# Fixed rows for the tokens routed last, and plain stores of the last output block

## The chip, the core and the metric

The kernel runs on one core of a Trainium2 chip. The core has five engines with an instruction queue each, and each queue runs strictly in order: TensorE (PE, matrix products), VectorE (DVE), ScalarE (ACT), GpSimd (POOL) and SyncE (SP, which here issues transfers). Engines wait for one another, and for transfers, by semaphores. The metric is the device time of one execution in microseconds (us); lower is better.

## The reference, cut to what matters

Attention over 4 sequences of 576 tokens, then a feed-forward in which each token goes to one of 8 experts, then a dense feed-forward with a squared relu. The 2304 output rows stand in the order of the tokens.

```python
x = attention(q, k, v, bias)                  # 2304 tokens x 512
expert_idx = np.argmax(logits, axis=1)        # one of 8 experts a token
for e in range(E):
    mask = expert_idx == e
    h = np.maximum(x[mask] @ w1[e], 0.0)
    out[mask] = gate_w[mask, None] * (h @ w2[e])
h = out @ w_in                                # 512 -> 2048
r = np.maximum(h, 0.0)
return (r * r) @ w_out                        # 2048 -> 512, 2304 rows
```

## The kernel before

**Stages.** Attention goes over 18 tiles of 128 tokens (`TILES`; the two last in the list are the tiles of chunk 3 of sequences 2 and 3). When a batch of tiles is done, `route` ranks its tokens within their experts and POOL scatters the token numbers into a list by expert, `id_d`. `base` holds the running count of tokens for each expert. `slots` cuts the list into slots of 128 tokens of one expert: 7 early slots (`NEARLY`) from the first 14 tiles, and then slots 7 to 21 (the compiled most is 30; what lies above 22 stands in a branch that these inputs don't take).

**The loop over slots** (`run_slots`, some 11 us a slot). For each slot POOL gathers the token numbers (`gather_id`, into `ti`), later the rows of x (`gather_x`, into `xg`), and splits x in two halves of 16 bits (`x_split`). PE transposes (`x_T`), multiplies with the expert's first matrix (`ff1`, two halves), and with the second (`ff2`). After each half of `ff1`, ACT and DVE make `h2` (DVE's line is L1226), and where the next slot has another expert they split new weights (`split_w1`). Between these stand the pieces of `convert`, which turns the dense weights into 16-bit pairs on ACT, DVE and POOL. The order on each engine is the order in which the code is written. In step `t` the code emits `gather_id(t + 6)`, `gather_x(t + 4)`, `ff1(t + 1)`, `x_T(t + 2)`, `x_split(t + 3)` and `ff2(t)`, in that order.

**Where a slot's results go.** `ff2_out` appends two numbers to each result row, a factor and the token's place in the output, and `y_out` stores the rows to `y_d`: early slots by SP in a plain transfer, later ones by POOL in an indirect transfer to the rows `yidx`, which closes the gaps that half-filled slots leave. So which token stands in which row of `y_d` depends on the data, and each row carries its place in the output with it.

**The dense feed-forward** goes over 9 blocks of 256 rows of `y_d`. `y_load` fetches them, `y_rows` takes out the factor (`meta`) and the place (`orow`), `g_unit` makes the hidden layer, and `ff2_of` the output in seven products of 24 matmuls into the PSUM tiles a, b, c, d. From these ACT and DVE (`comb`, L1465) put together two output tiles `o[0]` and `o[1]` of 128 rows x 512. `put` has POOL store each in an indirect transfer to the rows `orow` of the result (L1469):

```python
w = POOL.indirect_dma_start(out=out, out_offset=bass.IndirectOffsetOnAxis(ap=orow[:, t:t + 1], axis=0),
                            in_=o[i], in_offset=None, bounds_check=NT - 1, oob_is_err=False).ins
```

**The end of the program** (all under L1585): every engine runs a DRAIN and signals; SP first waits for the semaphore of every transfer; POOL collects the signals, clears the semaphores, and releases all.

Of the kernel before, what the change touches and what calls it, by code (L numbers as in the profile page):

```python
# [7 lines left out]
F32 = mybir.dt.float32  # L8
F16 = mybir.dt.float16
U32 = mybir.dt.uint32  # L10
I32 = mybir.dt.int32
AF = mybir.ActivationFunctionType
ALU = mybir.AluOpType
# [3 lines left out]

B, H, S, D = 4, 8, 576, 64
HID = 32
STEP, LIM = 1.95, 2.7  # L20
NT, DM = B * S, H * D
E, F1 = 8, 1024
F2 = 2048
P = 128
NP = H // 2
TILES = [(c, b) for c in (0, 1, 4, 2, 3) for b in ((0, 2) if c == 4 else range(B))]
NTILE = len(TILES)
NSLOT = NT // P + E - 1
NEARLY, TEARLY, NMOST = 7, 14, 22
XW, XX = DM + 2, DM + 3  # L30
# [53 lines left out]
def body(ctx: ExitStack, tc: tile.TileContext, q, k, v, wsm, emb, tau, mw1, mw2, win, wout, cst_d, lsk_d, ids_d, out):  # L84
    nc = tc.nc
    win, wout = win.bitcast(U32), wout.bitcast(U32)
    PE, ACT, DVE, POOL, SP = nc.tensor, nc.scalar, nc.vector, nc.gpsimd, nc.sync

    dram = ctx.enter_context(tc.tile_pool(name="dram", bufs=1, space=DRAM))
    cp = ctx.enter_context(tc.tile_pool(name="cp", bufs=1))  # L90
# [6 lines left out]
    x_d = dram.tile([NT + P, XX], F32, name="x_d")  # L97
# [11 lines left out]
    orow = cp.tile([P, NTILE], U32, name="orow")  # L109
    base = cp.tile([P, E], F32, name="base")  # L110
# [2 lines left out]
    w2s_c = cp.tile([P, 1], F32, name="w2s_c")  # L113
    basep = cp.tile([P, E], F32, name="basep")
    taken = cp.tile([P, E], F32, name="taken")
    xidx = cp.tile([P, NSLOT], U32, name="xidx")
    yidx = cp.tile([P, NSLOT], U32, name="yidx")
    tok = cp.tile([P, NTILE], U32, name="tok")
# [8 lines left out]
    def attention(actx, bctx, cctx, smp, mid, early, G):  # L127
        ap = lambda n, bufs, **kw: actx.enter_context(tc.tile_pool(name=n, bufs=bufs, side="right", **kw))
# [33 lines left out]
        def start(g, tag="B"):  # L162
            active.append([g, E_, tag])
# [460 lines left out]
        def route(bat):  # L624
            R = rbat.pop(bat)
            n = len(R["x"])
# [12 lines left out]
            ti = T("ti")  # L639
# [4 lines left out]
            z = T("z", E)  # L644
# [34 lines left out]
            if bat == (2, 0):  # L679
                DVE.tensor_copy(basep, base)  # L680
                start(early(), "A")
            ACT.activation(z, z, AF.Exp)
            yield E_
            DVE.tensor_tensor(out=rr, in0=rr, in1=oh, op=ALU.mult)
# [12 lines left out]
            for i, ti_ in enumerate(R["x"]):  # L697
                if i and (i == 2 or not soon):
                    yield E_

                put = POOL.indirect_dma_start(out=id_d, out_offset=bass.IndirectOffsetOnAxis(ap=ri[:, i:i + 1], axis=0),
                                              in_=tok[:, ti_:ti_ + 1], in_offset=None, bounds_check=E * NT * IW - 1,
                                              oob_is_err=False).ins
# [92 lines left out]
        for n in range(8, GR):  # L796
            c, i = divmod(n, 8)
# [61 lines left out]
    def slots(pool, fin):  # L859
        t0, n = (NEARLY, NSLOT - NEARLY) if fin else (0, NEARLY)  # L860
        tl = lambda shape, nm: pool.tile([P] + shape, F32, name="sl_" + nm)
        tn = lambda shape, nm: pool.tile([P, NSLOT - NEARLY] + shape, F32, name="sl_" + nm)[:, :n]
        ev8 = cst[:, C_E2304:C_E2304 + E]
# [3 lines left out]
        pcol = cst[:, C_P:C_P + 1]  # L867
        bc = lambda a: a.unsqueeze(1).to_broadcast([P, n, E])

        def below(x, nm):  # L870
            t2 = tl([E, E], "t2")
            DVE.tensor_tensor(out=t2, in0=x.unsqueeze(1).to_broadcast([P, E, E]), in1=tri8, op=ALU.mult)
            r = tl([E], nm)
            DVE.tensor_reduce(out=r, in_=t2, axis=AX.X, op=ALU.add)
            return r

        rem = tl([E], "rem")
# [23 lines left out]
        a = max(t0, 1)  # L901
# [31 lines left out]
            return  # L933

        DVE.tensor_scalar(live_i, cin[:, E - 1:E], float(NEARLY), None, op0=ALU.add)
        D = below(rem, "D")
        c128 = tl([E], "c128")
        DVE.tensor_scalar(c128, cex, float(P), None, op0=ALU.mult)
# [5 lines left out]
        DVE.tensor_scalar(tp, tt[:, :, 0], float(P), pcol, op0=ALU.mult, op1=ALU.add)  # L944
        DVE.tensor_tensor(out=R, in0=R, in1=tp, op=ALU.is_gt)
        DVE.scalar_tensor_tensor(out=Y, in0=tt[:, :, 0], scalar=float(P), in1=Y, op0=ALU.mult, op1=ALU.add)
        DVE.scalar_tensor_tensor(out=Y, in0=Y, scalar=float(NEARLY * P - NT), in1=R, op0=ALU.add, op1=ALU.mult)
        DVE.tensor_scalar(Y, Y, float(NT), pcol, op0=ALU.add, op1=ALU.add)
        DVE.tensor_copy(yidx[:, t0:t0 + n], Y)

    with tc.manual_schedule():
# [32 lines left out]
        def gather_x(t):  # L984
            a = G["xg"].tile([P, XX], F32, name="xg")
            n = TEARLY * P if t < NEARLY else NT + P
            POOL.indirect_dma_start(out=a, out_offset=None, in_=x_d[0:n, :],
                                    in_offset=bass.IndirectOffsetOnAxis(ap=ids.pop(t)[:, 0:1], axis=0),
                                    bounds_check=n - 1, oob_is_err=False)
            xg[t] = a  # L990

        def slot(t):
            ev[t] = SP.value_load(es_i[0:1, t:t + 1], min_val=0, max_val=E - 1)
# [53 lines left out]
        def early():  # L1047
            while "one" not in G:
                yield E_
            loaded = False  # L1050

            def first_loads():
                load_slot(0)

            for i, _ in enumerate(slots(G["one"], False)):
                if i > 3 and not loaded and "xs" in G:
                    first_loads()
                    loaded = True
                if i % 2:
                    yield E_  # L1060
            while "ids" not in G:
                yield E_
            gather_id(0)
            gather_id(1)
            while "xs" not in G:
                yield E_
            if not loaded:
                first_loads()
            yield E_
            gather_id(2)  # L1070
            gather_id(3)
            while "x" not in G:
                yield E_
            yield E_
            gather_x(0)
            gather_x(1)
            yield E_
            gather_x(2)
            gather_id(4)
            gather_id(5)  # L1080
            yield E_
            for kc in range(4):
                yield E_
                split_part(0, kc // 2, kc % 2)
                if kc < 3:
                    x_split(kc)
            while G["hs"] < HSW:
                yield E_
            for kc in range(4):
                load_w2(0, kc, True)  # L1090
            yield E_
            load_slot(1)
            turn(1, NMOST)
            yield E_
            load_slot(2)
# [162 lines left out]

        def y_rows(i, yr):
            DVE.tensor_copy(meta[:, i, :], yr[:, DM:XW])  # L1260
            DVE.tensor_copy(orow[:, i:i + 1], yr[:, DM + 1:XW])


        conv = pieces([convert(i, wrp) for i in range(NCONV)])
# [118 lines left out]
        with ExitStack() as fctx:  # L1383
# [64 lines left out]
            def ff2_of(j):  # L1448
                gt = gts.pop(j)
                m = [meta[:, 2 * j + i, 0:1] for i in range(2)]  # L1450
                bank = [pf2.tile([P, 512], F32, name=f"pf2_{x}")[:, :256] for x in "abcd"]
                pa, pb, pc, pd = bank
                o = [op_.tile([P, DM], F32, name=f"o{i}") for i in range(2)]
                u = lambda nm: up.tile([P, 256], F32, name=nm)

                def prod(ps, s, w, first, end):
                    i = 0
                    for c in range(8):
                        for a, b in ((0, 0), (0, 1), (1, 0)):
                            PE.matmul(ps, lhsT=gt[:, a, s, c, :], rhs=woh[:, c, b, w, :],  # L1460
                                      start=(i == 0 and first), stop=(i == 23 and end), skip_group_check=True)
                            i += 1

                def comb(dst, ps, i, x):
                    DVE.scalar_tensor_tensor(out=dst, in0=ps, scalar=m[i], in1=x, op0=ALU.mult, op1=ALU.add)  # L1465

                def put(i):
                    t = 2 * j + i
                    w = POOL.indirect_dma_start(out=out, out_offset=bass.IndirectOffsetOnAxis(ap=orow[:, t:t + 1], axis=0),  # L1469
                                                in_=o[i], in_offset=None, bounds_check=NT - 1, oob_is_err=False).ins  # L1470
                    for other in outs:
                        tc.declare_no_dep(w, other, reason="disjoint rows")
                    outs.append(w)

                prod(pa, 0, 0, True, False)
                s = [u(f"s{i}") for i in range(2)]
                for i in range(2):
                    ACT.activation(s[i], pa, AF.Copy, scale=m[i])
                yield
                prod(pb, 4, 4, True, True)  # L1480
                u2 = [u(f"u{i}") for i in range(2)]
                for i in range(2):
                    comb(u2[i], pb, i, s[i])
                yield
                prod(pc, 3, 3, True, False)
                u4 = u("u4")
                comb(u4, pc, 0, u2[0])
                yield
                prod(pd, 5, 5, True, False)
                comb(o[0][:, 256:], pd, 0, u4)  # L1490
                yield
                prod(pa, 2, 2, False, True)
                ACT.activation(o[1][:, :256], pa, AF.Copy, scale=m[1])  # L1493
                yield
                prod(pc, 6, 1, False, True)
                comb(o[1][:, 256:], pc, 1, u2[1])
                put(1)
                yield
                prod(pd, 1, 6, False, True)
                comb(o[0][:, :256], pd, 0, u2[0])  # L1500
                put(0)
                yield

            for g in range(8):
# [85 lines left out]
```

## Time and profile before

| | us |
|---|---|
| median of 3 runs (1011.03 to 1012.91) | 1011.57 |
| the profiled execution | 1017.84 |
| its span, first to last instruction | 1016.0 |
| PE, DVE, ACT, POOL busy in the span | 947.2, 662.3, 540.9, 497.0 |

The page gives busy times by engine, a chain of work that ended last, and groups of instructions; the trace behind it can be asked for a stretch, a line or an engine. DRAIN and semaphore instructions belong to an engine's sequencer (POOLq, SPq) and are not counted as busy, so a wait at the very end is not in the busy times. Instructions are named by line of the kernel before; a "releaser" is what ended an engine's idle time.

### The profile page before, as it was taken

The page shows a single profiled execution, that of the slowest core. Times are in us where ns is not written, and L with a number is a line of the kernel's source. Part 1 is how long each engine was busy: PE and PEld are TensorE (multiplying, and loading weights), DVE is VectorE, ACT ScalarE, POOL GpSimd, SP SyncE. Part 2 cuts the span into 40 slices and gives each one's busy share as a digit, 9 for nine tenths or more (in the row PEclk, how much of TensorE's full clock was granted, in tenths as well). Part 3 has the DMA queues.
Part 4 walks back from the last instruction along what each step waited for, and adds up shares of the span by engine and source line. Part 5 has one row for each costly group of instructions (what it writes and reads, how often), then busy time and mean ns, then how long its engine had stood idle before and what let it go on. Part 6 is the DMA issues. An engine that isn't in the chain of part 4 may idle for free. (4 is left out here: it accounts for less than half of the span.)

```text
span 1016.0 us, 24944 instructions
## 1 busy us (share of the span) xinstructions
PE 947.2 (93%) x9725; PEld 749.5 (74%) x9725; DVE 662.3 (65%) x1229; ACT 540.9 (53%) x1000; POOL 497.0 (49%) x415
## 2 busy tenths in 40 slices
PE   8687999999899879999989999999999999999995
PEld 4456776677577658777657667688888888888884
DVE  6665999988988664677866867245445455545441
ACT  6666777777777574455756665255323333333330
POOL 1213536437433352456637787266454554645541
PEclk9798999999999999999999999999999999999998
DMA  9988985998779343698898574362111111111001
GB/s 299 329 242 265 327 276 174 303 267 265 242 228 326 137 125 108 229 336 300 336 410 318 196 271 170 143 275 50 25 53 43 32 52 43 32 53 22 22 1 42
DMA packets 78844, 187.18 MB, mean 184 GB/s; under 512 B 26648, under 2 KB 26776, under 8 KB 76128
## 3 DMA queue, kind: packets, MB, share of 16 engines
q1 hardware_dynamic: 72656, 169.98, 50.1%
q0 software_dynamic: 6064, 15.54, 4.6%
q8 instruction: 78, 1.28, 0.6%
q14 instruction: 46, 0.38, 0.1%
HBM read 171.65 MB, written 51.73 MB: 220 GB/s over the span
## 5 line engine op out<-in xcount | busy, mean ns | idle before, releaser
L1438 POOL TENSOR_TENSOR gf<-gf 128x256 f32<-128x256 f32 x144 | 165.9, 1171 | 146.5 <-DVE gf L1435 124.5
L1422 PE MATMUL pf<-big,wih 128*128 128x256 f16 x1728 | 196.0, 273 | 1.7 <-PEq L1376 1.7
L1422 PEld LDWEIGHTS <-wih 128*128 128x128 f16 x1728 | 169.0, 98 | 21.6 <-issue 2.1
L1460 PEld LDWEIGHTS <-g 128*128 128x128 f16 x1512 | 147.4, 98 | 18.7 <-issue 1.0
L1428 ACT ACTIVATE gf<-pf 128x512 f32<-128x512 f32 x72 | 42.5, 597 | 193.5 <-PE pf L1422 135.7
L1220 PE MATMUL ph<-x,w1b 128*128 128x128 f16 x2112 | 125.6, 219 | 4.6 <-ACT x L1204 2.4
L1220 PEld LDWEIGHTS <-w1b 128*128 128x128 f16 x2112 | 120.6, 98 | 9.5 <-issue 4.4
L471 POOL TENSOR_TENSOR wh<-wr,w2s_c 128x1024 f16<-128x1024 f32 x32 | 61.4, 1918 | 132.4 <-DMA wr<-in_mw_dram 83.1
L1235 PE MATMUL py<-vt,h 128*128 128x512 f16 x528 | 119.0, 382 | 6.1 <-DMA vt<-wsc 6.1
L1446 DVE TENSOR_TENSOR g<-gf,g 128x1792 f16<-128x1792 f32 x36 | 85.5, 2375 | 50.2 <-ACT g L1445 50.2
L522 ACT ACTIVATE pr<-ssb,mn 128x576 f32<-128x576 f32 x144 | 111.8, 777 | 11.9 <-DVE mn L509 11.7
L509 DVE CUSTOM_DVE_ANT_0 ssb<-ps_s,bias 128x576 f32<-128x576 f32 x144 | 107.5, 749 | 4.6 <-DMA bias<-bias_d 2.5
L498 PE MATMUL ps_s<-kst,qd 128*128 128x288 f16 (+1 forms) x640 | 96.4, 291 | 14.0 <-DVE mn L509 9.5
L1435 DVE TENSOR_TENSOR gf<-gf 128x1024 f32<-128x1024 f32 x28 | 34.3, 1225 | 113.6 <-ACT gf L1428 113.6
L1235 PEld LDWEIGHTS <-h 128*128 128x128 f16 x528 | 51.1, 98 | 65.0 <-issue 8.6
L531 PE MATMUL ps_t<-cst,pr 128*128 128x128 f32 x576 | 92.7, 284 | 1.3 <-DVE pt L209 0.6
L556 PE MATMUL pv<-pt,vt 128*64 128x128 f32 (+1 forms) x1280 | 85.1, 276 | 8.0 <-DMA vt<-in_v_dram 5.7
L556 PEld LDWEIGHTS pv<-pt,vt 128*64 128x64 f32 x1280 | 67.6, 141 | 24.4 <-issue 18.2
L531 PEld LDWEIGHTS ps_t<-cst,pr 128*128 128x128 f32 x576 | 65.3, 145 | 24.8 <-issue 19.7
L498 PEld LDWEIGHTS <-qd 128*128 128x128 f16 (+1 forms) x640 | 56.4, 101 | 29.1 <-issue 18.5
L207 ACT COPY pt<-ps_t 128x512 f32<-128x512 f32 x99 | 57.1, 577 | 14.9 <-PE ps_t L531 11.0
L1445 ACT CAST g<-gf 128x1792 f16<-128x1792 f32 x36 | 60.3, 1676 | 4.3 <-POOL gf L1438 4.3
(194 smaller groups left out, 1547.8 us busy)
## 6 DMA issues: line engine op xcount, KB each, us to landing
vt<-wsc SPq DMA_DIRECT2D x88, 512.0 KB
wr<-in_mw_dram SPq DMA_DIRECT2D x76, 512.0 KB
kst<-in_mw_dram SPq DMA_DIRECT2D x44, 512.0 KB
wsc<-wh SPq DMA_DIRECT2D x32, 512.0 KB
bias<-bias_d SPq DMA_DIRECT2D x16, 576.0 KB
bias_d<-rt SPq DMA_DIRECT2D x28, 295.5 KB
qd<-qh SPq DMA_DIRECT2D x64, 128.0 KB
wr<-in_win_dram SPq DMA_DIRECT2D x8, 1024.0 KB
```

The source lines that it names most:

```text
L471: POOL.tensor_tensor(out=wh[:, 0], in0=wr, in1=w2s_c.to_broadcast([P, 1024]), op=ALU.mult)
L498: PE.matmul(s[r, hf, :288], lhsT=qd[:, h2, i, pr, r], rhs=kst[x - x % 2][:, pr, h2, x % 2, js], start=(i == 0), stop=(i == 1))
L509: DVE.tensor_tensor_reduce(out=ss.rearrange("p (a j) -> p a j", a=2), in0=s[:, :, :288], in1=btile[bkey[u]][:, h2].rearrange("p (a j) -> p ...
L522: ACT.activation(pr_sb[k_ // 2][:, h2], ssb.pop(k_), AF.Exp, bias=mns.pop(k_), scale=-1.0, accum_out=sums[c, b][:, h:h + 1])
L531: PE.transpose(pt_ps[k_][:, jc * P:(jc + 1) * P], src[:, j0:j0 + P], eye)
L556: PE.matmul(pv[o, cs], lhsT=vb[:, 2 * jc + h2, d] if jc < 4 else vb[o, 8, d], rhs=a[h2][:, jc, cs] if jc < 4 else e[o, cs], start=(jc == 0 ...
L1220: PE.matmul(p_[:, f4, :], lhsT=w[:, a, kc, f * P:(f + 1) * P], rhs=x2[:, b, kc, :], start=(i == 0), stop=(i == 11))
L1235: PE.matmul(p_, lhsT=h2[:, a, fc, :], rhs=wb2[fc // 2][:, b, fc % 2, :], start=(i == 0), stop=(i == 23))
L1422: PE.matmul(p_[:, h], lhsT=wih[:, a, kc, f * P:(f + 1) * P], rhs=y2[:, b, kc, :], start=(i == 0), stop=(i == 11))
L1438: POOL.tensor_tensor(out=g[:, d], in0=g[:, x], in1=g[:, y], op=op)
L1446: DVE.tensor_tensor(out=gt[:, 1, :, c:c + 2, :], in0=g[:, 1:8], in1=gt[:, 0, :, c:c + 2, :], op=ALU.subtract)
L1460: PE.matmul(ps, lhsT=gt[:, a, s, c, :], rhs=woh[:, c, b, w, :], start=(i == 0 and first), stop=(i == 23 and end), skip_group_check=True)
```

## The change

The 256 tokens of the two tiles routed last (`ZROW` is 2048, the row where they begin) keep fixed rows: token number `ti` goes to row `ti` of `y_d`. All other tokens close their gaps among themselves, for which `slots` counts them with `basez`, the counts before the last batch, in place of `base`. The number of the row is mended slot by slot: two DVE instructions behind each `gather_x` of slots 7 and on take `max(yidx, ti if ti >= ZROW else 0)`. Since the last block's rows are then known when the program is built, `put` stores that block's two tiles with SP in four plain transfers of 128 rows x 256, each as soon as its half is ready; the other eight blocks are scattered by POOL as before.

```diff
+            if bat == (3, 0):
+                DVE.tensor_copy(basez, base)
...
         DVE.tensor_scalar(live_i, cin[:, E - 1:E], float(NEARLY), None, op0=ALU.add)
+        DVE.scalar_tensor_tensor(out=rem, in0=taken, scalar=-float(P), in1=basez, op0=ALU.mult, op1=ALU.add)
+        DVE.tensor_tensor(out=rem, in0=rem, in1=ev8, op=ALU.subtract)
...
-        DVE.scalar_tensor_tensor(out=Y, in0=Y, scalar=float(NEARLY * P - NT), in1=R, op0=ALU.add, op1=ALU.mult)
-        DVE.tensor_scalar(Y, Y, float(NT), pcol, op0=ALU.add, op1=ALU.add)
+        DVE.tensor_scalar(Y, Y, float(NEARLY * P), pcol, op0=ALU.add, op1=ALU.add)
+        DVE.tensor_tensor(out=Y, in0=Y, in1=R, op=ALU.mult)
...
             xg[t] = a
+            if t >= NEARLY:
+                z, y = zid[:, t:t + 1], yidx[:, t:t + 1]
+                DVE.scalar_tensor_tensor(out=z, in0=ti, scalar=float(ZROW), in1=ti, op0=ALU.is_ge, op1=ALU.mult)
+                DVE.tensor_tensor(out=y, in0=y, in1=z, op=ALU.max)
...
-            DVE.tensor_copy(orow[:, i:i + 1], yr[:, DM + 1:XW])
+            if i * P < ZROW:
+                DVE.tensor_copy(orow[:, i:i + 1], yr[:, DM + 1:XW])
...
-                def put(i):
+                def put(i, ns=None):
                     t = 2 * j + i
+                    if t * P >= ZROW:
+                        ch, b = TILES[t]
+                        r0 = b * S + ch * P
+                        for n in (0, 1) if ns is None else (ns,):
+                            w = SP.dma_start(out=out[r0:r0 + P, 256 * n:256 * n + 256], in_=o[i][:, 256 * n:256 * n + 256]).ins
+                            for other in outs:
+                                tc.declare_no_dep(w, other, reason="disjoint rows")
+                        return
+                    if ns == 1:
+                        return
...
                 comb(o[0][:, 256:], pd, 0, u4)
+                put(0, 1)
...
                 comb(o[0][:, :256], pd, 0, u2[0])
-                put(0)
+                put(0, 0)
```

Three places show what moved. In the rows below, the line is that of the kernel it is taken from; in brackets stand the semaphores waited for, DMASW for a transfer that POOL issued, DMAHW for one that SP issued, the rest for an engine.

The end of POOL's queue before, behind its last arithmetic (`gf`, L1438): four scatters of 128 output rows, of block 7 and of block 8, then the common end.

```order
L1438 TENSOR_TENSOR gf<-gf 128x256
L1438 TENSOR_TENSOR gf<-gf 128x256 [waits Pool_49]
L1469 DMA out_dram<-o_14870,orow 2304x512 [waits DMASW4_49,DVE_49,Activation_49]
L1469 DMA out_dram<-o_14869,orow 2304x512 [waits DMASW5_49,DVE_49]
L1469 DMA out_dram<-o_15219,orow 2304x512 [waits DMASW6_49,DVE_49,Activation_49]
L1469 DMA out_dram<-o_15218,orow 2304x512 [waits DMASW7_49,DVE_49]
L1585 UNCONDITIONAL_BRANCH
L1585 ISA [waits barrier_Pool_Activation_PE_DVE_SP_gather]
```

The same place now:

```order
L1450 TENSOR_TENSOR gf<-gf 128x256
L1450 TENSOR_TENSOR gf<-gf 128x256 [waits Pool_49]
L1491 DMA out_dram<-o_14909,orow 2304x512 [waits DMASW4_49,DVE_49,Activation_49]
L1491 DMA out_dram<-o_14908,orow 2304x512 [waits DMASW5_49,DVE_49]
L1608 UNCONDITIONAL_BRANCH
L1608 ISA [waits barrier_Pool_Activation_PE_DVE_SP_gather]
```

The two scatters of block 8 are gone, and block 7's are POOL's last work.

The end of SP's queue before, where the last block's input (`ysr`) is transposed into `big`:

```order
L1411 DMA_TRANSPOSE big<-ysr 128x4x128 [waits DMAHW3_49,PE_49,Activation_49]
L1411 DMA_TRANSPOSE big<-ysr 128x4x128 [waits DMAHW4_49,DVE_49]
L1411 DMA_TRANSPOSE big<-ysr 128x4x128 [waits DMAHW5_49,Activation_49]
L1411 DMA_TRANSPOSE big<-ysr 128x4x128 [waits DMAHW6_49,DVE_49]
L1585 UNCONDITIONAL_BRANCH
```

The same place now:

```order
L1423 DMA_TRANSPOSE big<-ysr 128x4x128 [waits DMAHW3_49,PE_49,Activation_49]
L1423 DMA_TRANSPOSE big<-ysr 128x4x128 [waits DMAHW4_49,DVE_49]
L1423 DMA_TRANSPOSE big<-ysr 128x4x128 [waits DMAHW5_49,Activation_49]
L1423 DMA_TRANSPOSE big<-ysr 128x4x128 [waits DMAHW6_49,DVE_49]
L1485 DMA out_dram<-o_15257 128x256 [waits DMAHW7_49,DVE_49]
L1485 DMA out_dram<-o_15258 128x256 [waits DMAHW0_49,Activation_49]
L1485 DMA out_dram<-o_15258 128x256 [waits DMAHW1_49,DVE_49]
L1485 DMA out_dram<-o_15257 128x256 [waits DMAHW2_49,DVE_49]
L1608 UNCONDITIONAL_BRANCH
```

Four stores stand behind the last transposes, three of them waiting for DVE and one for ACT.

DVE's queue before, in step 5 of the loop over slots: the copy of two columns for the result row, two operations of `convert` (L1118, L1119), and `h2` of the next slot's first half.

```order
L1244 COPY ys<-ga 128x2 [waits DMAHW4_49,Pool_49]
L1118 TENSOR_SCALAR tb<-tb 128x1024 [waits Activation_49]
L1119 TENSOR_SCALAR tb<-tb 128x1024 [waits DVE_49]
L1226 SCALAR_TENSOR_TENSOR h_7319<-ph,h_7319 128x512 [waits Activation_49]
L1024 COMPARE_AND_BRANCH
L1015 SCALAR_TENSOR_TENSOR w1b<-kst_103,w1b 128x2x512 [waits DMAHW3_49,DMAHW2_49,Activation_49]
L1015 SCALAR_TENSOR_TENSOR w1b<-kst_103,w1b 128x2x512 [waits DMAHW5_49,DMAHW4_49,Activation_49]
```

The same place now:

```order
L1255 COPY ys<-ga 128x2 [waits DMAHW4_49,Pool_49]
L1129 TENSOR_SCALAR tb<-tb 128x1024 [waits Activation_49]
L1130 TENSOR_SCALAR tb<-tb 128x1024 [waits DVE_49]
L1000 SCALAR_TENSOR_TENSOR zid<-ti 128x1 [waits DMASW2_49]
L1001 TENSOR_TENSOR yidx<-yidx,zid 128x1 [waits DVE_49]
L1237 SCALAR_TENSOR_TENSOR h_7330<-ph,h_7330 128x512 [waits Activation_49]
L1035 COMPARE_AND_BRANCH
L1026 SCALAR_TENSOR_TENSOR w1b<-kst_105,w1b 128x2x512 [waits DMAHW3_49,DMAHW2_49,Activation_49]
L1026 SCALAR_TENSOR_TENSOR w1b<-kst_105,w1b 128x2x512 [waits DMAHW5_49,DMAHW4_49,Activation_49]
```

A pair of one-column operations stands ahead of `h2`, and its first waits for a transfer of POOL, the gather of `ti`. There are 15 such pairs, one for each of the slots 7 to 21.

## Rows read from the trace of the kernel before

**Rows 1.** Instructions of the program's end: duration ns min/median/max, first and last start

```profile
L1585 POOLq EVENT_SEMAPHORE  x4: 17/17/17, 1015.2 to 1015.9; - x4
L1585 POOLq DRAIN  x3: 40/113/9702, 1005.4 to 1015.7; - x3
L1585 SPq DRAIN  x3: 7/7/7, 1008.9 to 1015.4; - x3
L1585 PEldq DRAIN  x2: 13/1084/2155, 1002.8 to 1015.5; - x2
L1585 DVEq DRAIN  x2: 19/272/524, 1004.9 to 1015.4; - x2
```

**Rows 2.** What SP's queue waited for at the end: us in total, times, longest

```profile
SPq L1585 <- PEq L1585: 6.9, 2, 6.3
```

**Rows 3.** Timeline of the end: start us, us, engine, line, operation [idle before <-releaser]

```profile
990.47 0.97 POOL L1469 DMA_INDIRECT out_dram<-o,orow  x1 [0.30 <-issue]
...
1002.08 2.78 PE L1460 MATMUL pf_d<-woh,g 128*128 128x256 f16 x24
1002.28 0.48 DVE L1465 SCALAR_TENSOR_TENSOR o<-pf_c,meta,u 128x256 f32<-128x256 f32 x1 [4.76 <-PE pf_c L1460]
...
1004.90 0.48 DVE L1465 SCALAR_TENSOR_TENSOR o<-pf_d,meta,u 128x256 f32<-128x256 f32 x1 [2.14 <-PE pf_d L1460]
1005.66 0.97 POOL L1469 DMA_INDIRECT out_dram<-o,orow  x1 [1.16 <-DVE o L1465]
```

**Rows 4.** Stretches: us, PE, PEld, DVE, ACT, POOL busy, PEclk, DMA share, GB/s

```profile
643.40:644.10 0.70, 0.70 (x5) 0.34 (x4) 0.00 (x0) 0.70 (x2) 0.07 (x2) 1.00 0.00 0
644.10:645.20 1.10, 1.10 (x7) 0.51 (x6) 0.00 (x0) 1.10 (x1) 0.94 (x1) 1.00 1.00 417
...
1005.90:1007.10 1.20, 0.00 (x0) 0.00 (x0) 0.00 (x0) 0.00 (x0) 0.73 (x1) 1.00 0.00 0
1007.10:1008.10 1.00, 0.00 (x0) 0.00 (x0) 0.00 (x0) 0.00 (x0) 0.00 (x0) 1.00 0.69 262
```

**Rows 5.** SP's queue at 643 us, the stores of converted weights, 896 KB each

```profile
643.35 4.43 SPq L1144 DMA_DIRECT2D wosc<-wr  x2
```

**Rows 6.** DVE's timeline: two small dependent operations, and `h2` in two steps

```profile
411.39 0.16 DVE L879 SCALAR_TENSOR_TENSOR sl_rem<-taken,base 128x8 f32<-128x8 f32 x1
411.58 0.17 DVE L880 TENSOR_TENSOR sl_rem<-sl_rem,cst 128x8 f32<-128x8 f32 x1
...
447.46 0.69 DVE L1226 SCALAR_TENSOR_TENSOR h<-ph,h 128x512 f16<-128x512 f32 x1 [2.47 <-ACT h L1225]
...
458.39 0.69 DVE L1226 SCALAR_TENSOR_TENSOR h<-ph,h 128x512 f16<-128x512 f32 x1
```

**Rows 7.** POOL's timeline: gathers of token numbers for slots 8, 9 and 11

```profile
433.68 1.04 POOL L977 DMA_INDIRECT ti<-id_d,xidx  x1 [0.30 <-issue]
435.02 0.99 POOL L977 DMA_INDIRECT ti<-id_d,xidx  x1 [0.30 <-issue]
...
457.08 1.42 POOL L977 DMA_INDIRECT ti<-id_d,xidx  x1 [0.16 <-issue]
```

**Rows 8.** Busy time in the loop over slots, columns as in rows 4

```profile
430.00:655.00 225.00, 213.73 (x2406) 155.93 (x2405) 160.10 (x194) 127.52 (x157) 142.90 (x125) 0.99 0.76 277
```

**Rows 9.** What PE waited for, 430 to 655 us, columns as in rows 2

```profile
PE py L1235 <- DMA vt<-wsc: 6.1, 3, 3.4
...
PE ph L1220 <- ACT x L1204: 1.3, 2, 1.0
...
PE ph L1220 <- DVE w1b L1015: 1.0, 2, 0.6
```

**Rows 10.** What DVE waited for, 430 to 655 us, columns as in rows 2

```profile
DVE h L1226 <- ACT h L1225: 14.8, 9, 3.9
DVE h L1226 <- ACTq L1024: 13.4, 11, 2.5
```

More of the change, by code (lines that the diff above doesn't have):

```diff
@@ L27 @@
 NTILE = len(TILES)
+ZROW = (NTILE - 2) * P
 NSLOT = NT // P + E - 1
@@ L115, in body @@
     taken = cp.tile([P, E], F32, name="taken")
+    basez = cp.tile([P, E], F32, name="basez")
+    zid = cp.tile([P, NSLOT], U32, name="zid")
     xidx = cp.tile([P, NSLOT], U32, name="xidx")
@@ L986, in gather_x @@
             n = TEARLY * P if t < NEARLY else NT + P
-            POOL.indirect_dma_start(out=a, out_offset=None, in_=x_d[0:n, :],
-                                    in_offset=bass.IndirectOffsetOnAxis(ap=ids.pop(t)[:, 0:1], axis=0),
+            ti = ids.pop(t)[:, 0:1]
+            POOL.indirect_dma_start(out=a, out_offset=None, in_=x_d[0:n, :], in_offset=bass.IndirectOffsetOnAxis(ap=ti, axis=0),
                                     bounds_check=n - 1, oob_is_err=False)
             xg[t] = a
+            if t >= NEARLY:
+                z, y = zid[:, t:t + 1], yidx[:, t:t + 1]
+                DVE.scalar_tensor_tensor(out=z, in0=ti, scalar=float(ZROW), in1=ti, op0=ALU.is_ge, op1=ALU.mult)
+                DVE.tensor_tensor(out=y, in0=y, in1=z, op=ALU.max)
         def slot(t):
```

## The prediction

> **What bounds the kernel now.** I read the busy times first: PE works 947 of 1016 us, so an edit to a helper engine pays only where PE stands still. It stands still at the end, and for 11.3 us of the loop over slots, so I read those two places alone.
>
> At the end, the timeline [rows 3] shows PE's last product, DVE's last `comb` at 1004.90 (done at 1005.38) and POOL's last scatter from 1005.66 to 1006.63. The span goes on to 1016.0, and no engine is busy in those 9.4 us. The instructions of the program's end tell what fills them [rows 1]: POOL's DRAIN is one of 9.702 us that starts at 1005.4, so it ends at 1015.1. SP has seen every transfer land by its first DRAIN at 1008.9, and the other engines' DRAINs end before that. SP then stands 6.3 us for the common end [rows 2]. (The row puts that wait down to PE; PE's long DRAIN was over at 1005.) The rest, from POOL's first semaphore instruction at 1015.2 to the end, takes 0.8 us. So the end is set by POOL's DRAIN, 8.5 us behind POOL's last scatter, and not by the data.
>
> In the loop over slots PE is busy 213.7 of 225 us [rows 8]. Of what it waits for there, 6.1 us are weight transfers, and 2.3 us are four waits for ACT and DVE [rows 9].
>
> **The change part by part.**
>
> *POOL's DRAIN leaves the end.* POOL's last scatter is now that of block 7, done at 990.47 + 0.97 = 991.44 [rows 3]. If the DRAIN takes 9.7 us from there it ends at 1001.1; if 8.5 us, at 999.9. Either is over 4 us ahead of DVE's last result at 1005.38, so the last two products of PE cover it. Next in line is SP at 1008.9: the gain is 1015.1 - 1008.9 = 6.2 us. If that cover were gone, the DRAIN would be last again, and this gain with it. Bounds: 0, if the DRAIN stays at the end for another reason, and 6.3 [rows 2]. I take 6.2.
>
> *The last bytes land earlier.* Before, nothing moves from 1005.9 to 1007.1, and the 256 KB move from 1007.1 to 1008.1 [rows 4]: first bytes 1.7 us behind DVE's end, of which 0.28 us is POOL's start and 0.97 us its work on the scatter [rows 3]. A plain SP store has its price in the trace: issued at 643.35 [rows 5], nothing moves up to 644.1, and from there on the transfer engines are full at 417 GB/s [rows 4]. That is 0.75 us to the first bytes; with a tenth for the wait, 0.85 us in place of 1.7. The last piece is also a quarter of the block (128 KB), half of what the last scatter moved in 1.0 us: 0.4 us less. Sum: 1.2 us earlier. Bounds: 0.5 us later, if rows of 1 KB make a slow store (the store in the trace has 7 KB rows), and 1.6 us earlier. The three other stores are issued as their halves come, up to 1002.8, and SP has no other work, so the last finds it free.
>
> A rule of the Trainium skill ("Trainium Kernel Development and Optimization", Key Constraints) speaks against counting more than this: transfers issued from SP, ACT and POOL run on the same 16 DMA engines, and another issuer saves only the sequencer's issue time. By it the whole edit would be worth about what this paragraph gives, and POOL's DRAIN, which the rule doesn't know, would be worth nothing; that is 1010.7 us, the result of the first two rivals.
>
> *DVE gets 15 pairs in the loop over slots.* Two small dependent operations take 0.16 + 0.2 = 0.36 us [rows 6], 15 pairs 5.4 us, in a stretch where DVE has 65 us idle [rows 8]. Each pair stands ahead of `h2`. Where DVE comes to `h2` early, it then waits for ACT (28.2 us in 20 waits) [rows 10], and the pair falls into that wait. Where it comes late, as at 458.39 [rows 6], `h2` and the weight split behind it move by 0.36 us. PE needs both a step later, and only in two places was the split late for it, 1.0 us in all [rows 9]. Bounds: 0, and 5.4 us if every pair reaches PE. Four waits of PE for ACT or DVE that grow by 0.36 us each would be 1.4 us. I take 0.3 us, nearest to the first bound, since a wait of DVE lies ahead of most late stretches. A gain here is excluded, as nothing is taken off DVE in the loop.
>
> *The first of each pair waits for `ti`.* Behind it on DVE stand `h2`, the split and the conversion, and PE waits for these. But `gather_x` waits for the same numbers, and they are gathered two steps ahead: slot 9's at 435.02 [rows 7], and its pair would stand ahead of 458.39 [rows 6]. The closest are the first two pairs, for slots 7 and 8: slot 8's numbers are gathered at 433.68 [rows 7], and the pairs stand ahead of 447.46 [rows 6]. I put the wait at nothing; the cover is those two steps.
>
> *The rest* has one answer: one copy in the attention, two more operations in `slots` (0.36 us [rows 6], in a stretch whose following `h2` waits for ACT), two casts fewer in the last block. Zero.
>
> Sum: -6.2 - 1.2 + 0.3 = -7.1 us. The profiled execution would go from 1017.84 to 1010.7, its span from 1016.0 to 1008.9. The median lies 6.27 us under the profiled execution; I let it move by the same amount: 1011.57 - 7.1 = 1004.5.
>
> **The rivals.**
>
> *The DRAIN is long only under the profiler.* A DRAIN that long has no work in the trace to show for itself: the last bytes landed by 1008.1 [rows 4]. Without it the end would have been SP's 1008.9, 0.1 to signal, and 0.8: span 1009.8, and with the 1.84 us by which the profiled execution exceeds its span 1011.6. The median is 1011.57. That fits well, which speaks for this rival; but the profiler may as well cost 6 us over 25,000 instructions elsewhere. Against it: the other engines are profiled too, and their DRAINs take at most 2.2 us [rows 1], each no longer than the work ahead of it. Only POOL's is long, and POOL issues its transfers itself. Then the unprofiled runs gain the earlier landing alone: -1.2 + 0.3 = -0.9, 1010.7 us, within 0.2%. The Trainium skill ("Runtime: NRT & Kernel Launch", The ~15µs preamble/postamble breakdown) gives a constant gap of some 6.2 us between a profile's total and the runtime's own time; the 6.27 us here agree with its size, and no row shows where they lie.
>
> *The change doesn't do what it says.* The DRAIN may wait for the last landing of any transfer, SP's too: it ended 7.0 us behind the 1008.1 of rows 4. Then it moves with the landing, -1.2 + 0.3 again, 1010.7. Against it: POOL has nothing to do with SP's stores.
>
> *DVE is held by `ti`.* If POOL falls behind, DVE stands ahead of `h2` until the numbers land, and with it the split and PE. This is slower than before from 7.4/15 = 0.5 us a slot on; at the 1.4 us that POOL takes for a gather [rows 7] it would be 15 x 1.4 - 7.4, +13.6 us, 1025.2. Against it: 14 us and more between gather and use [rows 6, 7].
>
> **How the numbers follow.** Forecast, the DRAIN hidden: 0.66, at 1004.5, by its bounds from 1003.2 (a landing 1.6 us earlier, a tenth from the DRAIN, no cost on DVE, and 0.5 us for the scatter of runs) to 1006.5 (pairs at 1.4 us, landing 0.3 us earlier). DRAIN only profiled: 0.19, and moving with the landing: 0.05, both at 1010.7. Something between, part of the DRAIN left: 0.03. DVE held: 0.07. A measurement of this kernel can tell about 0.2% (2 us) from no change. So faster by more than that is 0.69, within it 0.24, slower 0.07. The range from 1003.2 to 1010.9 takes in the forecast, what lies between, and over half of the two rivals at 1010.7: 8 in 10. The forecast's own range is 1003.2 to 1006.5.
>
> **What would show it.** In the profile after: POOL's DRAIN starts at about 991 and ends by 1001; SP's DRAIN comes at about 1007.7, and the span ends within 1 us of it; no long SP wait at the end. The pairs take 0.36 us with no wait for a transfer ahead of them, and PE's waits for ACT and DVE in the loop stay under 4 us. If the profiled span falls by 7 us and the median by 1, the DRAIN was the profiler's. If the DRAIN still ends last, the second rival holds. A new wait of DVE for `ti`, longer than 0.5 us a slot, would make the forecast wrong on the other side.

## The result, and the profile after

| | before | after |
|---|---|---|
| median, us | 1013.06 (22 runs, 1006.69 to 1027.98) | 1004.18 (22 runs, 999.37 to 1013.22) |
| the profiled execution, us | 1017.84 | 1002.3 |
| its span, us | 1016.0 | 1000.4 |

The ratio of the times is 0.9912, with a 95% interval from 0.9892 to 0.9933: 8.9 us faster, between 6.8 and 10.9. The predicted time was 1004.5 us. The median of before over 22 runs lies 1.5 us above that of the three runs shown earlier; single runs lie as far as 14.9 us (before) and 9.0 us (after) from their median.

The two spans differ by 15.5 us, more than the medians do. I cut both at three points: PE's first product with an expert's weights, its first product of the dense feed-forward, and DVE's last result. The two lines of PE give the first two points. After "x" and a number stand min/median/max of one instruction in ns, then the first and the last start in us; the first row is of before, the other two are of after, and the last is again of before:

```profile
L1220 PE MATMUL ph<-x,w1b x2112: 216/219/230, 392.3 to 637.7; 128*128 128x128 f16 x192
```

```profile
L1231 PE MATMUL ph<-x,w1b x2112: 216/219/230, 385.7 to 630.4; 128*128 128x128 f16 x192
L1434 PE MATMUL pf<-big,wih x1728: 269/273/273, 642.0 to 969.5; 128*128 128x256 f16 x192
```

```profile
L1422 PE MATMUL pf<-big,wih x1728: 269/273/273, 650.0 to 977.4; 128*128 128x256 f16 x192
```

| stretch, us | before | after |
|---|---|---|
| start to the first product of an expert | 392.3 | 385.7 |
| from there to the dense feed-forward (loop over slots) | 257.7 | 256.3 |
| from there to DVE's last result | 355.4 | 355.4 |
| from there to the end of the span (the tail) | 10.6 | 3.0 |

The tail gives 7.6 us. The 6.7 us before the first expert are not the change's: a kernel below has the attention of before word for word, and there the same product starts at 396.1. Over nine traces with practically the same attention it starts anywhere from 385.7 to 396.1. The loop is 1.3 us shorter here, but goes from 256.3 to 258.4 us over the kernels below with one pair per slot or none.

The end of the program after answers to [rows 1] and [rows 2]. Instructions of the program's end, columns as there:

```profile
L1608 POOLq EVENT_SEMAPHORE  x4: 17/17/17, 999.6 to 1000.3; - x4
L1608 POOLq DRAIN  x3: 40/112/10232, 981.6 to 1000.2; - x3
L1608 SPq DRAIN  x3: 7/7/13, 999.5 to 999.9; - x3
```

And what SP's queue waited for there:

```profile
SPq L1608 <- DMA out_dram<-o: 1.0, 1, 1.0
SPq L1608 <- PEq L1608: 0.7, 2, 0.5
```

POOL's DRAIN is still long, 10.232 us, but starts at 981.6 and is over at 991.8. SP's first DRAIN now comes at 999.5, and POOL's first semaphore instruction follows it at once, at 999.6; the wait of 6.3 us of [rows 2] is gone. What SP waits for now is its own last store.

The timeline of the end, as [rows 3], shows what the DRAIN lies beside:

```profile
982.51 0.97 POOL L1491 DMA_INDIRECT out_dram<-o,orow  x1 [0.30 <-issue]
...
989.59 8.19 SPq L1485 DMA_DIRECT2D out_dram<-o  x4
991.50 2.78 PE L1472 MATMUL pf_c<-woh,g 128*128 128x256 f16 x24
...
994.12 2.78 PE L1472 MATMUL pf_d<-woh,g 128*128 128x256 f16 x24
...
996.94 0.48 DVE L1477 SCALAR_TENSOR_TENSOR o<-pf_d,meta,u 128x256 f32<-128x256 f32 x1 [2.14 <-PE pf_d L1472]
```

POOL's last scatter ends at 983.5, DVE's last result at 997.4. Between them stand five groups of PE's products, of 2.78 us each. And the stretches of the end, columns as in [rows 4]:

```profile
997.40:998.20 0.80, 0.00 (x0) 0.00 (x0) 0.03 (x1) 0.00 (x0) 0.00 (x0) 1.00 0.00 0
998.20:998.90 0.70, 0.00 (x0) 0.00 (x0) 0.00 (x0) 0.00 (x0) 0.00 (x0) 1.00 0.56 187
```

Nothing moves for 0.8 us behind DVE's end, then 187 GB/s for 0.7 us, 131 KB, which is the last store and all of it.

### The profile page after: what moved, and what is told of

It is laid out like the page before. It is cut to its first block, busy times and chain, and to the rows that moved or that the text cites. A ratio compares the mean times of both kernels' runs of the same rounds, so it can differ in the third digit from the quotient of the medians.

```text
span 1000.4 us, 24973 instructions
## 1 busy us (share of the span) xinstructions
PE 946.6 (95%) x9725; PEld 750.8 (75%) x9725; DVE 665.8 (67%) x1260; ACT 541.6 (54%) x1000; POOL 502.7 (50%) x413
## 5 line engine op out<-in xcount | busy, mean ns | idle before, releaser
L525 ACT ACTIVATE pr<-ssb,mn 128x576 f32<-128x576 f32 x144 | 111.7, 776 | 10.3 <-DVE mn L512 10.2
```

Source lines behind the costliest of these rows:

```text
L525: ACT.activation(pr_sb[k_ // 2][:, h2], ssb.pop(k_), AF.Exp, bias=mns.pop(k_), scale=-1.0, accum_out=sums[c, b][:, h:h + 1])
```

## The experiments

In those that follow, "the tail" is the stretch from DVE's last result to the end of the span. A ratio stands with its interval as it is on record; it is not always the quotient of the two medians beside it. Where only one run of a kernel is on record, no verdict rests on its time, and its trace is read for lengths alone.

**The stores alone.** The kernel before, with only the last block's four plain stores by SP; neither `basez` nor the pairs.

```diff
+                    if t * P >= ZROW:
+                        ...
+                            w = SP.dma_start(out=out[r0:r0 + P, 256 * n:256 * n + 256], ...)
+                        return
```

> The kernel before, with one part of the change: SP stores the last block in four plain transfers. The rows of y_d keep their old, closed order, so the last 256 rows of the result stand in other places than the reference's; the work is the same. My theory (the gain is the end of the program: POOL's DRAIN out of it, and an earlier landing): from the end of DVE's last comb to the end of the span 3.0 us, as after, against 10.6 before; POOL's DRAIN ends over 4 us ahead of DVE's last comb; time 7.4 us under before, 0.993. Rival (the profile after is shorter because of the fixed rows, or of something in the attention or the loop over slots): the tail is 3.0 all the same, but the time stays nearer to before, and the stretch up to the first dense product is as long as before's 650 us. The stretch itself varies from run to run by several us, so the verdict rests on the tail first and on the median of the runs next.

Measured: 1011.27 us against 1020.16 of the kernel before on that chip, ratio 0.9911, interval 0.9878 to 0.9944. The tail is 3.0 us: POOL's DRAIN is over at 1003.5, and the end follows SP's first DRAIN.

```profile
L1597 POOLq DRAIN  x3: 40/113/10230, 993.2 to 1011.8; - x3
L1597 SPq DRAIN  x3: 7/7/13, 1011.2 to 1011.5; - x3
```

Its first product of an expert is the late one told of above:

```profile
L1221 PE MATMUL ph<-x,w1b x2112: 216/219/229, 396.1 to 642.1; 128*128 128x128 f16 x192
```

So the four stores bring the whole gain.

**The rows alone.** The changed kernel with `basez` and the pairs, and POOL's scatters for the last block as before.

```diff
-                    if t * P >= ZROW:
-                        ...
-                        return
```

> The changed kernel with fixed rows and the 15 pairs on DVE, but the last block scattered by POOL as before. My theory: the tail is 10.6 us again, POOL's DRAIN ends 8.5 us behind POOL's last scatter and is last; the pairs cost 0.3 us (0 to 1.4), so the time is that of before within what can be told, 1.000 to 1.002. Rival (the pairs cost what DVE pays for them, 5.4 us): 1.005, and PE's waits for ACT and DVE in the loop over slots grow from 2.3 us to over 5. Rival (the layout is what gains): under 0.995.

Measured: 1018.99 us against 1020.16, ratio 0.9993, interval 0.9956 to 1.0030. The tail is 10.6 us, the loop 257.5. POOL's DRAIN is last again, and ends at 1011.8, 6.2 us behind SP's first:

```profile
L1596 POOLq DRAIN  x3: 40/112/9707, 1002.1 to 1012.3; - x3
L1596 SPq DRAIN  x3: 7/7/13, 1005.6 to 1012.0; - x3
```

The rest of the change brings nothing and costs nothing that shows.

**The last store by POOL, but plain.** Of the four stores POOL issues the last one.

```diff
-                            w = SP.dma_start(...
+                            w = (POOL if ns == 0 else SP).dma_start(...
```

(`ns` is 0 for the last of the four alone.)

> The changed kernel, with the last of the four stores issued by POOL, still a plain transfer of 128 rows x 256, and the other three by SP. My theory (the DRAIN runs on for 8.4 us behind the last transfer that POOL issues, whatever its kind): the DRAIN ends about 8.4 us behind the end of that store's work on POOL, and the tail is about 10 us again. Rival (it is the scatter, with its list of rows, that the DRAIN has to clear up): the DRAIN is over within 1 us, the tail is 3 to 4 us, and plain stores alone, by any engine, would have done.

POOL's timeline of the end, and the DRAINs of POOL and SP:

```profile
989.01 0.97 POOL L1491 DMA_INDIRECT out_dram<-o,orow  x1 [0.30 <-issue]
1004.23 0.60 POOL L1485 DMA_DIRECT2D out_dram<-o  x1 [14.25 <-DVE o L1477]
```

```profile
L1608 POOLq DRAIN  x3: 40/118/9048, 1004.2 to 1013.8; - x3
L1608 SPq DRAIN  x3: 7/7/13, 1006.9 to 1013.5; - x3
```

The DRAIN starts at 1004.2 and ends at 1013.25, 8.4 us behind the plain transfer of 0.60 us, and the tail is 10.2 us again. One run, 1015.94 us. So it is not the scatter that makes the end late; a plain transfer at the end of POOL's queue does it too.

**No scatter of the output at all.** All nine blocks stored by SP in plain transfers; POOL's last transfer is then one of the loop over slots.

```diff
-                    if t * P >= ZROW:
-                        ch, b = TILES[t]
-                        r0 = b * S + ch * P
+                    if True:
+                        r0 = t * P
```

> The changed kernel with all 18 output tiles stored by SP in plain transfers, in the order of y_d's rows; so the rows of the first eight blocks stand in other places than the reference's. POOL's last transfer is then the scatter into y_d at about 650 us, and POOL works on for over 300 us without one. My theory (the DRAIN's time counts from POOL's last transfer): POOL's DRAIN at the end of its queue takes under 1 us. Rival (a DRAIN of POOL is 8 us and more once POOL has issued transfers, whenever): it takes 8 to 10 us from where POOL reaches it, as in the profile after, hidden there. The tail is 3.0 us in both.

POOL's last instructions, and its DRAINs:

```profile
980.28 4.56 POOL L1450 TENSOR_TENSOR gf<-gf 128x256 f32<-128x256 f32 x4 [3.31 <-DVE gf L1447]
```

```profile
L1607 POOLq DRAIN  x3: 40/113/8374, 983.5 to 1008.8; - x3
```

My theory was that the DRAIN counts from POOL's last transfer, which ends here at 654.2. It fell: the DRAIN is still 8.374 us long, and ends 7.0 us behind POOL's last addition, 338 us behind its last transfer. One thing was left: 7.0 us here, 8.3 to 8.5 elsewhere. This kernel has 16 scatters fewer than the changed one.

**How long the DRAIN is, by itself.** Five small kernels without any of the computation: SP stores zeros; POOL issues a number of plain transfers and runs 24 products of some 1.04 us each. They differ in one loop (32 transfers of 128 rows; for the fourth 8 rows each, for the fifth 96 transfers of 128 short rows) and in the size of the tensor that it writes. In the third all 32 go to the same rows, so each waits for the one before, the products run between them, and a transfer ends POOL's queue; in the others the products end it:

```diff
-    for _ in range(0):
+    for _ in range(32):
         POOL.dma_start(out=d, in_=a)
```

> All of the computation is left out: SP stores zeros, and POOL runs 24 small products and issues no transfer. Theory A (POOL's DRAIN is long once POOL has issued transfers in the program): without any, its DRAIN ends within 1 us of POOL's last product. Theory B (the DRAIN of POOL is long whatever POOL did): 8 to 10 us as in the whole kernel. Theory C (it grows with the number of POOL's transfers): short here.

> As the kernel with no transfer of POOL, with one plain transfer issued by POOL ahead of the 24 products. Theory A: DRAIN of 8 to 10 us, as in the whole kernel. Theory B: the same, 8 to 10 us. Theory C: not longer than without a transfer by more than some tenths.

> As the kernel with no transfer of POOL, with 32 plain transfers issued by POOL. Theory A and theory B: 8 to 10 us, as with one. Theory C: several times as long as with one transfer; the whole kernel issues some 100 and has 9.7 us, so between 1 and 9 us.

> All of the computation is left out: SP stores zeros, POOL issues 32 plain transfers of 8 rows, each to rows of its own, and then runs 24 small products. From the runs so far the end of POOL's DRAIN behind its last instruction is 8.50, 8.42, 8.34 and 7.05 us with 103, 102, 101 and 85 transfers of POOL in the program, 0.081 us for each and 0.18 us besides. Theory (it goes by the number of transfers): 0.18 + 32 x 0.081 = 2.8 us. Rival (it goes by rows moved, which were nearly always 128 a transfer): a sixteenth of that, 0.3 us. Second rival (the last transfers being unfinished when the queue ends made the 3.4 us of the kernel with 32): under 0.3 us, since 25 us of products stand behind the transfers here.

> As the kernel with 32 short transfers, with 96 plain transfers of 128 rows of 128 bytes. Theory (0.081 us for each transfer): POOL's DRAIN ends 0.18 + 96 x 0.081 = 8.0 us behind the last product. By rows: 8.0 us too. By bytes (the whole kernel's 101 move 15 MB, these move 1.6 MB): under 1.5 us.

POOL's DRAINs of the program's end, for none, 1, 32, 32 short and 96 transfers, and below each POOL's last instructions from its timeline:

```profile
L163 POOLq DRAIN  x3: 34/76/1142, 27.5 to 29.1; - x3
```

```profile
1.80 26.76 POOL L99 TENSOR_TENSOR b<-b 128x512 f32<-128x512 f32 x24
```

```profile
L163 POOLq DRAIN  x3: 34/88/1232, 28.2 to 29.9; - x3
```

```profile
2.48 26.77 POOL L99 TENSOR_TENSOR b<-b 128x512 f32<-128x512 f32 x24
```

```profile
L163 POOLq DRAIN  x3: 40/101/3597, 96.3 to 100.4; - x3
```

```profile
96.00 0.54 POOL L97 DMA_DIRECT2D d<-a  x1 [2.04 <-DMA d<-a]
```

```profile
L163 POOLq DRAIN  x3: 34/101/3776, 47.3 to 51.5; - x3
```

```profile
21.56 26.77 POOL L99 TENSOR_TENSOR b<-b 128x512 f32<-128x512 f32 x24
```

```profile
L163 POOLq DRAIN  x3: 40/101/9002, 78.6 to 88.1; - x3
```

```profile
52.90 26.77 POOL L99 TENSOR_TENSOR b<-b 128x512 f32<-128x512 f32 x24
```

The DRAIN's row starts before POOL's last instruction has ended, so what counts is how far it ends behind that instruction. For 96 transfers that is 78.6 + 9.0 - (52.90 + 26.77) = 7.9 us, although the last of them was issued 27 us before POOL's queue ended. The number of POOL's transfers in the whole kernel is the sum of these groups of the changed kernel (line, operation, names, count, busy us, mean ns, idle before), 22 + 15 + 22 + 18 + 16 + 8 = 101:

```profile
L984 POOL DMA_INDIRECT ti<-id_d,xidx x22 | 29.8, 1355 | 12.2 <-issue 4.0 <-DVE sl_rem L941 3.8 <-DVE sl_cex L936 3.4
...
L1264 POOL DMA_INDIRECT y_d<-ys,yidx x15 | 25.0, 1666 | 20.9 <-DMA wr<-in_mw_dram 9.2 <-DVE tb L1129 6.5 <-DVEq L1388 3.5
...
L995 POOL DMA_INDIRECT xg<-x_d,ti x22 | 24.4, 1108 | 8.2 <-issue 5.4 <-PE ps_r L594 2.4 <-PE ps_t L534 0.3
...
L706 POOL DMA_INDIRECT id_d<-tok,ri x18 | 18.7, 1041 | 33.5 <-DVE se L700 14.2 <-DVE rs L597 12.3 <-issue 3.1
L1491 POOL DMA_INDIRECT out_dram<-o,orow x16 | 15.7, 984 | 11.7 <-issue 10.5 <-DVE o L1477 1.1
...
L290 POOL DMA_DIRECT2D qd<-qh x8 | 4.6, 586 | 23.8 <-DVE qh L283 23.8
```

The kernels beside one another, the end of the DRAIN behind POOL's last instruction taken from the trace's times to the hundredth:

| POOL's transfers in the program | what ends POOL's queue | DRAIN ends behind it, us | 0.065 + 0.082 x count |
|---|---|---|---|
| 0 | product | 0.07 | 0.07 |
| 1 | product | 0.16 | 0.15 |
| 32, 8 rows each | product | 2.70 | 2.69 |
| 32, 128 rows each | transfer | 3.38 | 2.69 |
| 85 (no scatter of the output) | addition | 7.05 | 7.04 |
| 96, 128 short rows each | product | 7.93 | 7.94 |
| 101 (after) | scatter | 8.34 | 8.35 |
| 102 (last store by POOL) | plain store | 8.42 | 8.43 |
| 103 (before) | scatter | 8.50 | 8.51 |

The five other traces give the same: 8.50 us for the rows alone (103 transfers), and 8.34 to 8.36 us for the four others with 101. One line holds for nearly all: 0.082 us for each transfer that POOL issued since the program began. Rows and bytes don't enter: 32 transfers of 8 rows lie on the same line as the whole kernels, and 96 transfers of 16 KB take as long, each for each, as the whole kernel's. Of the rivals, "long once POOL has issued a transfer" falls by 0.16 us for one, "always long" by 0.07 us for none. The one off the line, 0.7 us above it, has transfers that each wait for the one before, up to the end of the queue; what adds this stays open. An unfinished last transfer alone doesn't: in before and in the kernel with the last store by POOL it is unfinished too when POOL's queue ends, and both lie on the line. But there SP has seen it land over 6 us before the DRAIN ends, here 0.8 us before; which of this matters was not tried. What POOL does in the DRAIN no row shows.

**POOL's queue ends late without a transfer.** The changed kernel with one POOL addition that waits for the last output piece.

```diff
+                        if (i, ns) == (0, 0):
+                            POOL.tensor_tensor(out=u("late"), in0=o[i][:, :256], in1=o[i][:, :256], op=ALU.add)
```

> The changed kernel, with one POOL addition of 128 x 256 that waits for the last output piece, so that POOL's queue ends late again, without a transfer. Theory (the DRAIN runs some 7 to 8.5 us from the end of POOL's queue, whatever ends it): POOL's DRAIN ends 7 to 9 us behind that addition, the stretch from DVE's last result to the end of the span is 9 to 11 us in place of 3.0, and the span is 6 to 8 us longer than with the addition left out. Rival (the time belongs to POOL's last scatter, which was 15 us earlier): the stretch stays within 1 us of 3.0.

```profile
1006.92 0.61 POOL L1489 TENSOR_TENSOR late<-o 128x256 f32<-128x256 f32 x1 [14.03 <-DVE o L1477]
```

```profile
L1610 POOLq DRAIN  x3: 40/113/9005, 1006.9 to 1016.5; - x3
```

An addition of 0.61 us brings the tail back to 9.9 us: the DRAIN ends at 1015.9, 8.36 us behind it, as 101 transfers want. So the DRAIN runs from the end of POOL's queue, whatever ends it. The kernel's one run took 1018.62 us.

**Six pairs in place of one.**

```diff
+                for _ in range(6):
                     DVE.scalar_tensor_tensor(out=z, in0=ti, ...)
                     DVE.tensor_tensor(out=y, in0=y, in1=z, op=ALU.max)
```

> The changed kernel with six pairs per slot in place of one: 75 pairs of some 0.36 us more, 27 us more of DVE's time in the loop over slots. Theory (a pair falls into a wait of DVE or of PE's cover): most of it is hidden; the loop, 256 to 258 us from the first product of an expert to the first of the dense feed-forward, grows by 0 to 8 us, and PE's waits for DVE in it grow by as much. Rival (each pair reaches PE): 27 us longer. The stretch from DVE's last result to the end of the span stays at 3.0 us in both.

Measured: 1013.46 us against 1014.72 of before on that chip, ratio 1.0001, interval 0.9951 to 1.0052; no gain over before can be told. The tail is 3.0 us, as expected. The loop is 265.0 us, 7.6 more than the mean of the five traces with one pair (257.4), with 27 us more of DVE's work. What PE waited for, 380 to 675 us:

```profile
PE ph L1232 <- DVEq L1036: 5.8, 3, 2.4
PE py L1247 <- DMA vt<-wsc: 4.6, 2, 2.6
PE ph L1232 <- DVE w1b L1027: 3.2, 5, 0.8
...
PE ph L1232 <- DVE h L1238: 0.6, 1, 0.6
```

In the changed kernel DVE stood in PE's way in that stretch for 1.2 us, here for 5.8 + 3.2 + 0.6 (a wait for `h2`). So about a quarter of what is added reaches PE, 0.10 us a pair; the theory's upper end was just reached, and the rival's 27 us are far.

**The pair ahead of its time.** The pair moved right behind `gather_id`, two steps earlier.

```diff
         def gather_id(t):
             ...
+            if t >= NEARLY:
+                DVE.scalar_tensor_tensor(out=z, in0=ti, ...)
+                DVE.tensor_tensor(out=y, in0=y, in1=z, op=ALU.max)
```

> The changed kernel with the pair moved right behind the gather of the slot's token numbers, so that DVE has to stand until that gather has landed, 15 times. Theory (the two steps between gather and use are the cover that makes the wait cost nothing): the first operation of the pair now waits 2 to 5 us in many slots, and the loop over slots grows by 3 to 25 us from its 256 to 258 us. Rival (a wait of DVE there costs nothing either, since DVE waits for ACT behind it anyway): the loop stays at 256 to 259 us.

Measured: 1027.93 us against 1014.72, ratio 1.0144, interval 1.0108 to 1.0180. What DVE waited for ahead of the pair, and what PE waited for behind it, 380 to 675 us:

```profile
DVE zid L992 <- DMA ti<-id_d,xidx: 39.5, 11, 8.7
```

```profile
PE ph L1231 <- DVEq L1035: 6.0, 3, 4.7
PE ph L1231 <- DVE w1b L1026: 4.5, 8, 0.8
...
PE ph L1231 <- DVE h L1237: 4.1, 2, 2.9
```

DVE stands 39.5 us, 3.6 us at a time, and the loop is 273.4 us, 16 us longer. The two steps between gather and use are the cover, and this is what it is worth.

## Why the prediction was right, point by point

**The DRAIN leaves the end: right.** SP's first DRAIN was 6.2 us ahead of the end of POOL's, and these 6.2 us are gone. The prediction had two lengths for the hidden DRAIN, 8.5 us behind POOL's last scatter or 9.7 us long; it ends 8.3 us behind it, 5.6 us ahead of DVE's last result, where "over 4" was expected. (All times of the end lie some 8 us earlier than the prediction names them, since the dense feed-forward starts at 642.0 in place of 650.0.) The reason was incomplete. I took the 8.5 us as something that belongs to the end of a scatter; they are 103 times 0.082 us, and any late instruction of POOL's would have held the end as the scatter did. The forecast of the 6.2 us came out because the change clears POOL's queue of everything late, not of its scatter alone.

**The last bytes land earlier: right, 1.45 us in place of 1.2.** SP's first DRAIN stood 3.56 us behind DVE's end and stands 2.11 us behind it now. The 0.85 us to the first bytes, taken from the plain store of [rows 5] and [rows 4], are what the stretches of after show; the quarter of the block moves in at most 0.7 us. The fear that rows of 1 KB make a slow store had no ground. Together with the DRAIN: 7.6 us of tail, where 7.4 were predicted.

**The pairs: +0.3 us, within what can be told.** Most pairs take the 0.36 us that were predicted, but three, between 561 and 589 us, take 0.9 to 1.4 us. In the rows of the two operations, after the count, stand min/median/max in ns:

```profile
L1000 DVE SCALAR_TENSOR_TENSOR zid<-ti x15: 141/149/698, 435.7 to 598.0; 128x1 uint32<-128x1 uint32 x15
L1001 DVE TENSOR_TENSOR yidx<-yidx,zid x15: 159/159/722, 435.8 to 598.2; 128x1 uint32<-128x1 uint32 x15
```

The loop takes 257.7 and 257.6 us in the two kernels without pairs, and 256.3, 257.5, 258.4, 256.6 and 258.1 in five with one pair per slot. At the 0.10 us per pair that the six-pair kernel shows, 15 would cost 1.5 us; the difference of the means is -0.2, and single traces differ by 2. What PE waited for in the loop, 430 to 655 us, to be held against [rows 9]:

```profile
PE py L1246 <- DMA vt<-wsc: 5.0, 3, 3.3
PE ph L1231 <- DVE w1b L1026: 1.2, 2, 0.6
PE px L1214 <- POOL xs L1049: 1.1, 2, 0.7
PE ph L1231 <- ACT x L1215: 1.0, 1, 1.0
```

Its waits for ACT and DVE are 2.2 us, under the 4 us named.

**No wait for `ti`: right.** The trace of after has no idle time of DVE ahead of the pair's first operation, and the kernel with the early pair shows what stood to lose: 16 us of loop, 1.07 us a slot, near the 1.4 us of the rival that ended slower. Against before on its chip it is 13.2 us slower by the medians (by the interval 11 to 18), and that rival had 13.6; but the loop and the tail account for 16.0 - 7.6 = 8.4 us of it, and where the rest lies is not shown, so this nearness is chance.

**The sum.** -7.1 us predicted, -7.6 us in the tail, -8.9 us by the medians, with an interval from -6.8 to -10.9 in which both lie. That the measured 1004.18 us came within 0.4 us of the 1004.5 is luck: the median started from was 1.5 us too low, and the gain by the medians 1.8 us larger than forecast.

**The rivals.** The DRAIN as something of the profiler's had 0.19. By it the timed runs would have gained 0.9 us; they gained 8.9. Its evidence was a fit: span 1009.8 plus 1.84 equals the median. The fit was chance. Every execution of the two kernels that has a span on record took 1.8 to 1.9 us longer than that span; the profiled execution of after, 1002.3 us, is itself the first of the 22 timed ones and lies under their median. So no cost of the profiler lies between profiled and timed executions, and the 6.27 us between the profiled execution of before and the median of three runs are the scatter of runs, of which three showed too little (1011.03 to 1012.91, where 22 go from 1006.69 to 1027.98). The step that failed is the reading of that gap, in which I saw a cost of the profiler as possible. Whether an execution of which nothing at all is recorded would have the same DRAIN, no run here shows. The Trainium skill ("Runtime: NRT & Kernel Launch", The ~15µs preamble/postamble breakdown) has a constant gap of some 6.2 us between a profile's total and the runtime's time. No run here shows it; what the runs have is the 1.8 to 1.9 us between a time and its span, and the agreement with the 6.27 us was chance too.

That the DRAIN waits for the last landing of any transfer is refuted: it ends at 991.8, and the last store lands at about 999. The Trainium skill's rule ("Trainium Kernel Development and Optimization", Key Constraints) that another issuer saves only the issue time would have left 1010.7 us. For the landing alone the traces don't speak against it: SP's first DRAIN stands 2.96 us behind DVE's end when POOL issues the last plain store (1006.89 less 1003.93) and 2.11 us when SP does, and POOL's start and work on that store are 0.30 + 0.60 us. But with that store POOL's the tail is 10.2 us, and with SP's 3.0. Who issues the last transfer mattered by 7 us, of which some 0.85 are the later landing and the rest the end of the issuer's queue.

## What to carry to other kernels

Read the end of a program as a stretch of its own: the instructions of the common end tell which engine signs off last, and that engine's queue need not be the one whose data came last. Where POOL issues many transfers, let its queue run dry early: in these kernels the end costs it 0.082 us for each transfer of the whole program, and this lies beside other work only if nothing of POOL's, not even one small addition, stands at the end. Before a gap between a profiled time and a median of three is put down to a cause, ask how far single runs scatter.

## What the runs showed of the hardware

POOL's DRAIN at the end grows with the number of transfers that POOL issued, by 0.082 us each, from 0.07 us with none to 8.5 us with 103; neither rows, bytes, kind (plain or indirect) nor the time since the last one enters. And the same attention took from 385.7 to 396.1 us up to the first product of an expert in nine traces, while the stretches behind it, with the same work, differ by 2 us; so most of the scatter of these traces lies there, and what makes it differ stays open.
